# Wider transposes, a u product over two tiles and bias rows on ScalarE, in a retention and gated-MLP kernel bound by TensorE

## The chip, the cores and the metric

The kernel runs on one core of a Trainium2 chip. The metric is the device time of one execution in microseconds (us); lower is better. The kernel before takes 233.5 to 236 us, depending on which chip and in which set of runs. A time below is the median of the runs of its set, slow ones (over 1.5% above the fastest of the same kernel) included. Most sets also ran the kernel before on the same chip in turn with the new one, and only such ratios, of the means of fast runs alone, are compared across sets.

Engines are named as the profile does: PE is TensorE doing matmuls, PEld is TensorE loading weights, DVE is VectorE, ACT is ScalarE, POOL is GpSimd, SP is SyncE, which starts the loads and stores (SPq in the page's list of DMA issues).

## The reference

Eight sequences of 576 positions and eight heads of width 64 go through causal retention (scores weighted by a power of a decay per head, no softmax). The result, 512 wide, goes through a gated MLP whose gate mixes along the sequence.

```python
def _attn_ref(q, k, v):                       # (8, 8, 576, 64) each
    scores = scale * np.matmul(q, k.transpose(0, 1, 3, 2))
    Dmat = np.where(rel >= 0, gamma[:, None, None] ** rel[None, :, :], 0.0)
    return np.matmul(scores * Dmat[None], v)

def _moe_ref(x, w_in, g_ln, w_sg, b_sg, w_out):   # x: (8, 576, 512)
    h = gelu_tanh(x @ w_in)                   # d_ff 1024
    u, v = h[..., :512], h[..., 512:]
    v_n = layernorm(v) * g_ln
    v_s = np.einsum('ts,bsd->btd', w_sg, v_n) + b_sg[None, :, None]
    return x + (u * v_s) @ w_out
```

(Shortened: the decay, the gelu and the layer norm are written by name.)

## The kernel before

The work is cut into blocks of 256 positions (two tiles of 128) and single blocks, five to a pair of sequences. Per block: load q, k, v; multiply q and v by decay factors (GpSimd); transpose q and k on PE; scores, masks, state and output of the retention; then the MLP's hv (the v half), hu (the u half), wp (the product along the sequence) and op (the output). Names in the profile are these tile names; pp is the PSUM tile of transposes, scores and retention output.

A job is one such piece on one engine. A list of job numbers, found beforehand by a search against a timing model, gives the order of issue on each engine. The parts that the change touches:

```python
# transposes: one per 64x64 tile; R picks the input half, C the output half
for a in (1, 0):
    for kk in range(KK):
        for s in range(ns):
            o = ((a * KK + kk) * ns + s) * 64
            for r in range(2):
                for c in range(2):
                    R, C = slice(64 * r, 64 * r + 64), slice(64 * c, 64 * c + 64)
                    ins = nc.tensor.transpose(tpf[C, r, o:o + 64], qkb[R, s, a, KK * c + kk, :], ident[R, R])

# u: one job for one tile of 128 positions, 16 matmuls of 128 columns
for c in range(KK):
    for kk in range(KK):
        ins = nc.tensor.matmul(hu[:, c, :], w_in[:, kk, 128 * c:128 * c + 128],
                               xTs[p][:, kk, 128 * m:128 * m + 128], start=(kk == 0), stop=(kk == KK - 1), ...)

# bias rows: six small copies on VectorE
for t in vmid:
    nc.vector.tensor_copy(t[0][NB0:NB0 + 4, :], row4b[:, 0, :F2])
    nc.vector.tensor_copy(t[1][0:4, :], row4b[:, 0, :F2])

# what a job of u waits for: the half of xT that holds its tile
xd = [J["x", b, s]] if ns == 2 else [J["x", b, 0], J["x", b, 1]]
```

Of the kernel before, what the change touches and what calls it, by code (L numbers as in the profile page):

```python
# [18 lines left out]
OVL = {"PE": 0.0, "DVE": 60.0, "ACT": 90.0, "POOL": 50.0, "SP": 0.0}  # L19
SWITCH = {("F", "Q"): 93.0, ("Q", "F"): 125.0}  # L20
# [4 lines left out]
    '1 0 2 80 81 6 82 f9 83 7 84 f4 85 111 112 87 8 88 f3 114 86 113 3 115 9 89 118 283 120 12 116 119 284 285 286 '  # L25
    '117 23 121 90 f6 287 123 122 288 124 289 13 290 f6 304 127 305 125 4 5 306 126 307 f3 291 128 296 292 15 11 10 '
    '16 308 293 14 297 309 129 294 310 298 17 311 312 301 295 24 315 313 136 303 314 320 25 316 299 302 130 321 317 '
    '18 132 19 32 133 318 20 f3 319 134 21 131 135 22 34 322 300 327 325 328 326 105 329 91 330 137 106 93 323 33 92 '
    '331 94 324 109 332 99 138 110 139 35 100 333 103 97 334 104 98 336 26 366 140 335 101 27 367 95 145 337 107 36 '
    '102 368 108 143 37 141 96 369 144 f1 338 147 342 339 38 355 343 344 142 346 146 356 370 347 154 148 345 28 371 '  # L30
    '387 149 372 340 353 373 341 41 374 31 354 29 150 152 30 151 155 379 40 375 350 388 153 380 156 357 39 351 376 '
    '381 389 358 352 157 163 43 390 437 158 391 377 438 44 392 396 384 378 161 397 159 162 165 439 49 385 401 440 160 '
    '386 398 402 52 164 393 399 441 172 394 166 395 42 174 458 442 167 459 348 443 382 444 349 58 400 445 383 170 403 '
    '446 168 171 460 46 360 461 190 404 169 48 363 405 361 447 414 45 364 179 421 415 450 422 362 406 173 451 47 462 '
    '407 452 479 175 480 463 365 416 464 181 176 359 423 465 51 417 466 424 53 412 455 467 410 413 180 468 408 456 '
    '448 411 457 50 409 469 449 453 188 470 474 454 182 57 475 189 520 183 177 521 471 54 431 178 472 473 186 432 481 '
    '522 187 476 482 433 523 418 484 483 199 477 541 184 191 419 185 542 488 420 478 206 56 192 485 489 524 55 486 '
    '195 487 197 525 425 527 196 526 533 426 207 528 427 534 531 198 529 530 428 532 490 535 200 429 591 538 491 201 '
    '193 430 434 194 592 492 540 496 539 493 543 497 435 593 436 204 594 544 205 494 546 217 498 545 208 495 60 555 '
    '499 61 550 59 556 552 551 612 553 202 209 66 613 203 547 210 500 548 64 507 549 511 508 554 62 595 512 501 213 '  # L40
    '557 596 614 214 597 502 615 513 224 602 559 503 65 598 599 603 604 73 215 600 558 509 601 222 536 605 510 606 '
    '568 537 514 569 609 560 515 216 564 611 561 516 223 218 72 565 610 633 211 219 231 562 634 212 63 577 78 575 578 '
    '616 563 67 576 220 617 221 674 619 517 618 79 625 675 518 620 626 232 519 225 621 68 635 676 226 636 677 240 566 '
    '638 70 637 607 622 567 229 608 627 234 233 572 230 642 235 573 630 574 639 643 242 632 579 631 238 227 580 239 '
    '695 640 241 623 581 696 641 570 249 624 71 504 228 69 628 571 74 505 644 582 629 506 645 76 588 583 678 589 584 '
    '236 679 745 590 237 681 251 646 746 663 680 647 690 664 250 682 691 650 683 747 651 697 748 684 243 698 766 244 '
    '265 699 687 767 700 704 688 247 267 705 689 768 245 769 701 248 709 702 692 246 654 710 648 703 694 749 655 693 '
    '649 252 750 253 258 585 260 661 586 652 751 662 587 259 685 75 653 752 77 706 686 787 707 254 256 255 788 658 '
    '257 656 659 753 660 657 770 708 266 754 261 755 771 711 668 772 262 773 671 276 669 713 670 268 712 263 828 269 '
    '756 672 829 673 264 720 757 731 721 714 732 729 715 270 730 830 789 271 831 274 724 777 725 722 778 275 718 723 '  # L50
    '716 719 761 717 758 762 736 759 760 739 737 763 738 733 740 741 764 779 734 774 765 735 780 782 775 742 783 776 '
    '272 781 743 790 849 792 273 665 744 784 850 791 796 666 785 667 832 786 277 833 797 278 793 834 726 835 794 841 '
    '727 795 728 836 842 798 281 837 279 282 844 799 839 280 845 800 840 838 815 801 851 816 843 806 852 807 846 808 '
    '853 810 854 809 858 848 811 847 855 859 860 856 804 857 861 817 805 863 862 818 802 865 864 825 803 867 812 826 '
    '866 827 822 813 872 814 823 874 873 824 878 875 868 879 870 869 819 871 887 820 821 880 888 889 876 881 883 877 '
# [9 lines left out]
class Job:  # L65
    def __init__(self, eng, dur, due, fn, deps=(), new=None, uses=(), mode=None, nbytes=0, run=0, what="", behind=None, since=0.0, lag=0.0):
        self.what, self.behind, self.since, self.lag = what, behind, since, lag
        self.eng, self.dur, self.due, self.fn = eng, dur, due, fn
        self.deps = [d for d in deps if d is not None]
        self.new = [] if new is None else list(new) if isinstance(new, (list, tuple)) else [new]  # L70
        self.mode, self.nbytes, self.run = mode, nbytes, run
        self.start = self.out = None
        for b in uses:
            b.users.append(self)
        for b in self.new:
            b.users.append(self)


class Planner:


    def __init__(self, bufs, free, slack=60.0, penalty=500.0, fill=None, fill_until=0.0):
# [5 lines left out]
        self.mode, self.warm = None, False  # L88

# [5 lines left out]
    def ready(self, j):  # L95
        t = max(self.free[j.eng], j.since)
        if j.behind is not None:
            if j.behind.start is None:
                return None
            t = max(t, j.behind.start + 100.0)  # L100
# [23 lines left out]
    def place(self, j, t):  # L124
# [15 lines left out]
        else:  # L140
            j.out = t + j.dur
            self.free[j.eng] = t + j.dur - OVL[j.eng]
# [69 lines left out]
def kernel(  # L212
# [64 lines left out]
    garg = consts.tile([128, 2, NBK * 2, H], F32, name="garg")  # L277
    gqv = consts.tile([128, 2, NBK * 2, H], F32, name="gqv")
# [16 lines left out]
    for h in range(H):  # L295
        nc.vector.tensor_scalar(garg[:, 0, :, h], srow[:].rearrange("p n s -> p (n s)"), lng[h], lsc,
                                op0=Alu.mult, op1=Alu.add)
    nc.vector.tensor_scalar(garg[:, 1, :, :], garg[:, 0, :, :], -1.0, lsc, op0=Alu.mult, op1=Alu.add)
    nc.scalar.activation(gqv[:].rearrange("p a m h -> p (a m h)"), garg[:].rearrange("p a m h -> p (a m h)"), Act.Exp)
# [9 lines left out]
    def fill(n, cold):  # L309
# [6 lines left out]
        return Job("PE", 216.0 * n + cold, 0.0, f, new=bf, mode="F")  # L316
# [16 lines left out]
    def win_load(half):  # L333
# [15 lines left out]
        for a, eng, dur in ((0, "DVE", 690.0), (1, "ACT", 1060.0)):  # L349
            jw[half, a] = add(eng, dur, 0.0, lambda a=a, eng=eng: g(a, eng), deps=[ld], uses=[bf], what=("winc", half, a))  # L350
# [40 lines left out]
    st = {}  # L391
# [17 lines left out]
    def a_prep(b, t):  # L409
# [3 lines left out]
        src = f_[:, :, :ns * D].rearrange("p h (s d) -> p s h d", s=ns)  # L413
        if t in "qk" and (b, "qkb") not in st:
            st[b, "qkb"] = new("qkb", [128, 2, 2, H, D], BF)
        if t == "k":
            if b == 0:
                nc.scalar.activation(st[b, "qkb"][:, :ns, 1], src, Act.Copy)
            else:
                nc.gpsimd.tensor_copy(st[b, "qkb"][:, :ns, 1], src)  # L420
            return
        if t == "v":
            st[b, "vb"] = new("vb", [128, 2, H, D], BF)
            dst = st[b, "vb"][:, :ns]
        else:
            dst = st[b, "qkb"][:, :ns, 0]
        a = 0 if t == "q" else 1
        eng = nc.vector if b == 0 and t == "q" else nc.gpsimd
        for s in range(ns):
            eng.tensor_tensor(dst[:, s], src[:, s],  # L430
                                    gqv[:, a, 2 * n + s, :].unsqueeze(2).to_broadcast([128, H, D]), op=Alu.mult)
# [25 lines left out]
    def a_T(b):  # L457
# [7 lines left out]
        for a in (1, 0):  # L465
            for kk in range(KK):
                for s in range(ns):
                    o = ((a * KK + kk) * ns + s) * 64
                    for r in range(2):
                        for c in range(2):  # L470
                            R, C = slice(64 * r, 64 * r + 64), slice(64 * c, 64 * c + 64)
                            ins = nc.tensor.transpose(tpf[C, r, o:o + 64], qkb[R, s, a, KK * c + kk, :], ident[R, R])  # L472
                            n += 1
                            if n == 4:
                                mark(ins, ("T", b))
# [49 lines left out]
    def a_Z(b, c, first):  # L525
# [7 lines left out]
        for kk in range(KK):  # L533
            for s in range(ns):
                for hh in range(2):
                    ins = nc.tensor.matmul(z[64 * hh:64 * hh + 64, kk, :], st[b, "qkb"][R, s, 1, KK * hh + kk, :],  # L536
# [96 lines left out]
    def m_stats(i, first, slot):  # L633
        if first:
            cur["mv"] = new("mv", [128, 2, 4], F32)
        mvs[i] = (cur["mv"], slot)
        bst = sb.tile([128, 6], F32, name="bst", tag="bst", bufs=3)
        nc.vector.bn_stats(bst[:], vgs[i][:])  # L638
        nc.vector.bn_aggr(cur["mv"][:, slot, 0:2], bst[:])  # L639
# [21 lines left out]
    def m_U(i):  # L661
        p, m = divmod(i, NT)
        if m == 0:
            uTs[p] = new("uT", [128, KK, NT * 128], BF)
        hu = psD.tile([128, KK, 128], F32, name="hu", tag="d")
        cur["hu", i] = hu
# [338 lines left out]
```

## Time and profile before

| | before |
|---|---|
| time | 234.21 us (3 runs, 232.78 to 237.35) |
| PE busy | 88% of 233.9 us |
| PE instructions in the built program | 8927, of which 2304 are transposes with their loads and 1152 are u with its loads |
| holes on PE that the prediction puts down to instruction fetch | 9.85 us, ten holes |
| first wp product, last end on PE | 44.83 us, 228.76 us |

The prediction below shows the page's totals, the holes and the blocks of 256 instructions. First the page's PE and clock digits in 40 slices of 5.85 us (9 is 90% or more; the clock is the share of full speed that was granted):

```profile
PE   6638988869869998999989979999999999999991
PEclk9997999997999999999999999999999999999999
```

The clock stands at 7 in two slices. The second, from 52 us, is this stretch in the windows view (stretch, length, busy time and count of PE, PEld, DVE, ACT, POOL, then granted clock, DMA share, GB/s):

```profile
52.00:55.40 3.40, 3.18 (x12) 1.51 (x10) 1.52 (x3) 2.59 (x5) 3.10 (x4) 0.50 1.01 247
55.40:58.00 2.60, 2.60 (x45) 1.50 (x45) 2.04 (x2) 1.47 (x3) 0.00 (x0) 1.00 0.31 87
```

For 3.40 us TensorE ran at half speed, and then at full speed again. By my estimate that lost half of the stretch, 1.7 us. PE's timeline (start, length, engine, line, operation, out<-in, rows*columns of the array, sizes, count, and in brackets the idle time before it):

```profile
48.12 0.62 PE L557 MATMUL pp<-ret,vb 64*64 64x128 bf16 x32
48.57 0.59 PE L472 MATMUL pp<-ident,qkb 64*64 64x64 bf16 x49
51.01 0.32 PE L472 MATMUL pp<-ident,qkb 64*64 64x64 bf16 x15 [1.85 <-issue]
```

The first row ends at 48.74 and the second starts at 48.57: they overlap by 0.17 us, so transposes follow the other 64x64 matmuls without a stop. The transposes are then cut after 49 of 64.

### The profile page before, as it was taken

To read this page: it belongs to the slowest core of one execution; us is meant where nothing else is said; L and a number is where in the kernel's file an instruction comes from. 1 tells how busy PE (TensorE), PEld (TensorE's weight loads), DVE (VectorE), ACT (ScalarE), POOL (GpSimd) and SP (SyncE) were. 2 spreads that over 40 slices of the span, in tenths; PEclk is the share of its full clock that TensorE was granted. 3 is DMA by queue.
4 is the path that set the end of the run, shared out by engine and by line. 5 is a ranking of instruction groups with operands and counts; after the bars stand their busy time and mean duration, and the time that the engine had idled before them with its cause. 6 is when DMAs were issued, how large, how long until landed. Compare 5 with 4: busy or idle time off the path is not lost.

```text
span 233.9 us, 9967 instructions
## 1 busy us (share of the span) xinstructions
PE 205.4 (88%) x4428; PEld 145.1 (62%) x4463; DVE 135.7 (58%) x246; ACT 134.6 (58%) x235; POOL 118.1 (51%) x188
## 2 busy tenths in 40 slices
PE   6638988869869998999989979999999999999991
PEld 1326567654647685668657666677768757667660
DVE  6995746855457746567647484368487416654320
ACT  3013996526567665778376537767655378865431
POOL 5480378984644992976088298457447022222000
PEclk9997999997999999999999999999999999999999
DMA  6999999996498996432997896960262032100333
GB/s 166 290 352 244 259 252 278 337 245 158 134 272 210 301 310 182 117 125 94 298 303 161 218 312 193 238 221 3 81 193 95 0 137 92 48 3 0 135 137 137
DMA packets 70062, 42.88 MB, mean 183 GB/s; under 512 B 14138, under 2 KB 63298, under 8 KB 70018
## 3 DMA queue, kind: packets, MB, share of 16 engines
q1 hardware_dynamic: 70000, 42.23, 65.0%
q8 instruction: 35, 0.57, 1.1%
q14 instruction: 9, 0.07, 0.1%
q10 hardware_dynamic: 18, 0.00, 0.0%
HBM read 32.79 MB, written 9.44 MB: 181 GB/s over the span
## 4 chain that ended last, share of the span: by engine, by line
PE 75%; ACT 7%; DVE 7%; issue 7%; POOL 1%; POOLq 0%; ACTq 0%; DVEq 0%
PE wp L687 17%; PE hu L669 12%; PE op L713 12%; PE hv L624 11%; PE pp L557 6%; PE pp L472 5%; PE op L708 4%; PE pp L504 3%; PE zp L536 3%; PE wtp L782 1%; ACT vg L631 1%; ACT xT L613 1%; PE scr L315 1%; DVE bst L638 1%; DVE ret L517 1%
## 5 line engine op out<-in xcount | busy, mean ns | idle before, releaser
L517 DVE TENSOR_TENSOR ret<-pp,msk 128x1024 bf16<-128x1024 f32 x32 | 38.2, 1216 | 22.4 <-PE pp L504 22.4
L430 POOL TENSOR_TENSOR vb<-ld,gqv 128x512 bf16<-128x512 f32 x36 | 37.3, 1053 | 10.5 <-DMA ld<-in_v_dram 6.1
L687 PE MATMUL wp<-wT,vn 128*128 128x288 bf16 x256 | 41.4, 290 | 0.4 <-ACT uT L678 0.4
L430 POOL TENSOR_TENSOR qkb<-ld,gqv 128x512 bf16<-128x512 f32 x34 | 34.8, 1043 | 13.5 <-DMA ld<-in_q_dram 7.6
L697 DVE TENSOR_TENSOR uT<-wp,uT 128x288 bf16<-128x288 f32 x64 | 28.3, 451 | 20.2 <-PE wp L687 19.0
L669 PE MATMUL hu<-xT,w_in 128*128 128x128 bf16 x576 | 37.5, 219 | 2.8 <-issue 2.8
L669 PEld LDWEIGHTS <-w_in 128*128 128x128 bf16 x576 | 33.9, 98 | 6.5 <-issue 3.6
L613 ACT ACTIVATE xT<-pp 128x512 bf16<-128x512 f32 (+1 forms) x40 | 24.9, 673 | 20.3 <-PE pp L557 20.3
L638 DVE BATCH_NORM_STATS2 bst<-vg 128x6 f32<-128x512 f32 x36 | 24.7, 686 | 20.4 <-ACT vg L631 20.3
L624 PE MATMUL hv<-w_in,xT 128*128 128x512 bf16 x126 | 34.6, 385 | 1.7 <-issue 0.5
L713 PE MATMUL op<-w_out,uT 128*128 128x512 bf16 x130 | 34.3, 379 | 1.3 <-issue 0.5
L481 DVE COPY qkT<-pp 128x2048 bf16<-128x2048 bf16 (+1 forms) x20 | 22.3, 1113 | 20.5 <-PE pp L472 20.3
L643 POOL TENSOR_SCALAR mv<-mv 128x2 f32<-128x2 f32 (+1 forms) x20 | 4.5, 224 | 58.4 <-DVE mv L639 30.0
L718 ACT ACTIVATE ob<-op 128x512 f32<-128x512 f32 x36 | 21.1, 594 | 19.8 <-PE op L713 19.8
L678 ACT ACTIVATE uT<-hu 128x512 bf16<-128x512 f32 x36 | 21.3, 595 | 17.4 <-PE hu L669 17.3
L687 PEld LDWEIGHTS <-vn 128*128 128x128 bf16 x256 | 24.6, 99 | 9.0 <-issue 0.6
L631 ACT ACTIVATE vg<-hv 128x512 f32<-128x512 f32 x36 | 21.3, 595 | 11.5 <-PE hv L624 7.4
L658 ACT ACTIVATE vn<-vg,mv 128x512 bf16<-128x512 f32 x32 | 24.9, 809 | 3.5 <-POOL mv L646 3.4
L420 POOL CAST qkb<-ld 128x1024 bf16<-128x1024 f32 (+1 forms) x19 | 17.9, 949 | 8.8 <-DMA ld<-in_k_dram 4.7
L624 PEld LDWEIGHTS <-xT 128*128 128x128 bf16 x144 | 13.2, 99 | 13.3 <-ACT xT L613 1.0
L545 ACT ACTIVATE zb<-zp 128x256 bf16<-128x256 f32 x32 | 12.2, 381 | 15.8 <-PE zp L536 13.0
L687 PE MATMUL wp<-wT,vmid 128*128 128x288 bf16 x64 | 18.7, 292 | 0.0
(78 smaller groups left out, 253.6 us busy)
## 6 DMA issues: line engine op xcount, KB each, us to landing
out_dram<-ob SPq DMA_DIRECT2D x36, 256.0 KB, 2.2
ld<-in_k_dram SPq DMA_DIRECT2D x16, 512.0 KB, 7.3
ld<-in_q_dram SPq DMA_DIRECT2D x16, 512.0 KB, 7.9
ld<-in_v_dram SPq DMA_DIRECT2D x16, 512.0 KB, 7.2
wst<-in_moe_w_in_dram SPq DMA_DIRECT2D x2, 1024.0 KB
wst<-in_moe_w_sg_dram SPq DMA_DIRECT2D x2, 576.0 KB, 4.0
ld<-in_q_dram SPq DMA_DIRECT2D x8, 128.0 KB, 4.6
ld<-in_k_dram SPq DMA_DIRECT2D x8, 128.0 KB, 4.6
```

Of the source, the lines that this page charges most:

```text
L430: eng.tensor_tensor(dst[:, s], src[:, s], gqv[:, a, 2 * n + s, :].unsqueeze(2).to_broadcast([128, H, D]), op=Alu.mult)
L481: ins = nc.vector.tensor_copy(st[b, "qkT"][:].rearrange("p c a k t -> p c (a k t)")[:, :, :w], st.pop((b, "tp"))[:].rearrange("p c a k s t ...
L517: ins = nc.vector.tensor_tensor(ret[:].rearrange("p r (k t) -> p (r k) t", k=2), sc[:].rearrange("p r (k t) -> p (r k) t", k=2), msk2[:].r ...
L613: nc.scalar.activation(dst, src, Act.Copy)
L624: ins = nc.tensor.matmul(hv[:], xTs[p][:, kk, 128 * m:128 * m + 128], w_in[:, kk, F2:], start=(kk == 0), stop=(kk == KK - 1))
L631: unfence(nc.scalar.activation(vgs[i][:], cur.pop(("hv", i))[:], Act.Gelu_apprx_tanh), ("V", i))
L638: nc.vector.bn_stats(bst[:], vgs[i][:])
L658: nc.scalar.activation(vn[:], vg[:], Act.Identity, scale=mv[:, s, 2:3], bias=mv[:, s, 3:4])
L669: ins = nc.tensor.matmul(hu[:, c, :], w_in[:, kk, 128 * c:128 * c + 128], xTs[p][:, kk, 128 * m:128 * m + 128], start=(kk == 0), stop=(kk ...
L687: ins = nc.tensor.matmul(ps[:], vns[t0 + j][e][:, 128 * c:128 * c + 128], wT[e][j][:, half * HS:(half + 1) * HS], start=(j == 0), stop=(j ...
L697: ins = nc.vector.tensor_tensor(uTs[p][:, c, col:col + HS], cur.pop(("wp", b, c, half))[:], uTs[p][:, c, col:col + HS], op=Alu.mult)
L713: ins = nc.tensor.matmul(op[:], uTs[p][:, c, r], w_out[:, c, :], start=False, stop=(c == KK - 1), skip_group_check=True)
```

## The change

Four things are meant to make PE's program shorter and its start earlier.

- A transpose takes 64 rows and 128 columns of weights (two heads) at a time: half as many. q and k are laid out for that when they are prepared.
- u is computed for both tiles of a block in one matmul of 256 columns. One job makes half of the channels for two tiles.
- The bias rows are placed by ScalarE.
- The order is searched again, with a model that counts PE's instructions and charges 4.8 us for each block of 256.

```diff
+FETCH = 4800.0
+            if j.eng == "PE":
+                while self.count + j.ins > 256 * self.block:
+                    at = t + j.dur * (256 * self.block - self.count) / j.ins + late
+                    late += max(0.0, self.landed - at)
+                    self.landed = max(self.landed, at) + FETCH
...
                     for r in range(2):
-                        for c in range(2):
-                            R, C = slice(64 * r, 64 * r + 64), slice(64 * c, 64 * c + 64)
-                            ins = nc.tensor.transpose(tpf[C, r, o:o + 64], qkb[R, s, a, KK * c + kk, :], ident[R, R])
+                        R = slice(64 * r, 64 * r + 64)
+                        ins = nc.tensor.transpose(tpf[:, r, o:o + 64], qkb[R, a, kk, s].rearrange("p c d -> p (c d)"), ident[R, R])
...
-    def m_U(i):
+    def m_U(i, w, half):
+        cs = range(KK) if w == 1 else range(2 * half, 2 * half + 2)
+        for n, c in enumerate(cs):
             for kk in range(KK):
-                ins = nc.tensor.matmul(hu[:, c, :], w_in[:, kk, 128 * c:128 * c + 128],
-                                       xTs[p][:, kk, 128 * m:128 * m + 128],
+                ins = nc.tensor.matmul(hu[:, n, :], w_in[:, kk, 128 * c:128 * c + 128],
+                                       xTs[p][:, kk, 128 * m:128 * m + 128 * w],
...
+        xd = [J["x", b, 0], J["x", b, 1]]
...
         for t in vmid:
-            nc.vector.tensor_copy(t[0][NB0:NB0 + 4, :], row4b[:, 0, :F2])
-            nc.vector.tensor_copy(t[1][0:4, :], row4b[:, 0, :F2])
+            nc.scalar.activation(t[0][NB0:NB0 + 4, :], row4b[:, 0, :F2], Act.Copy)
+            nc.scalar.activation(t[1][0:4, :], row4b[:, 0, :F2], Act.Copy)
```

(Left out are the order list, the new layout of the decay factors and of q and k, the other row copies, and bookkeeping of the u jobs.)

## The prediction

The sum: -0.7 (u) - 7 (fetch) + 4 (modes) - 2 (bias rows) - 1.5 (order) = -7.2, so 234.2 became 227.0 us. In rival (1) "near 232" stands without support, and of rival (4), slower writes of GpSimd, nothing in the trace spoke; the 0.04 for "slower" rested on it alone. A mode is the shape of the array that the timeline prints for a matmul (128*128, 64*128 or 64*64). A drain is the overlap that is missing where the mode changes: 0.08 us at the change quoted, for 0.16 to 0.20 between neighbours of one mode. What PE does there no trace shows. The 56 ns of a 128-column step is the usual one; the shortest in the trace is 55.

> **What bounds the kernel now.** I read the page first, then the groups by shape, the chain in order of time, and the windows and timeline around its waits.
>
> ```profile
> PE 205.4 (88%) x4428; PEld 145.1 (62%) x4463; DVE 135.7 (58%) x246; ACT 134.6 (58%) x235; POOL 118.1 (51%) x188
> DMA  6999999996498996432997896960262032100333
> q8 instruction: 35, 0.57, 1.1%
> PE 75%; ACT 7%; DVE 7%; issue 7%; POOL 1%; POOLq 0%; ACTq 0%; DVEq 0%
> ```
>
> The first line is each engine's busy time and instruction count, the second the DMA share in 40 slices of 5.85 us, the third one row of the DMA queues, the last the chain that ended last. TensorE is the bound: 75% of the chain (some 175 us) is matmuls, no other engine is over 58% busy, and after about 55 us the timeline shows PE almost without a hole. Before that the DMA digits stand at 9, PE runs fill matmuls, and the start is set by loads and by VectorE. "Issue", 7% or some 16 us, is time in which PE waited for no semaphore. The long pieces of it (start us, us, what):
>
> ```profile
> 43.15 1.11 issue
> 49.16 1.85 issue
> 62.31 0.94 issue
> 68.24 1.75 issue
> 117.55 1.04 issue
> 136.12 1.16 issue
> ```
>
> With 0.74 at 91.74, 0.32 at 95.89, 0.55 at 142.67 and 0.39 at 158.80 they sum to 9.85 us. What they are, the windows from the end of one such hole to the start of the next show (columns: stretch, length, PE and PEld busy with counts, then DVE, ACT, POOL, clock, DMA share, GB/s):
>
> ```profile
> 44.20:49.15 4.95, 4.89 (x128) 3.77 (x128) 3.64 (x7) 0.72 (x1) 4.75 (x5) 1.00 1.05 295
> 63.20:68.20 5.00, 4.90 (x127) 3.61 (x128) 2.37 (x3) 3.88 (x7) 3.61 (x4) 1.00 1.02 278
> 92.45:95.60 3.15, 3.07 (x125) 2.38 (x127) 1.24 (x2) 2.73 (x7) 2.98 (x6) 1.00 0.25 91
> ```
>
> Each stretch holds 128 + 128 = 256 instructions, a few records missing. PE stops after 256 instructions, in the middle of a job: the hole at 49.16 cuts the 64 transposes of one block into 49 and 15. And the instruction queue moved 35 packets in 0.57 MB, 16.4 KB or 256 x 64 bytes each, for 4428 + 4463 = 8891 PE instructions, which are 35 blocks. So these 9.85 us are **instruction fetch**. A block plus its hole took 4.95 + 1.85 = 6.8 us with the DMA full, but 3.15 + 0.32 = 3.5 us with it a quarter busy.
>
> [...] neighbours of one mode overlap by 0.16 to 0.20 us, the full-array matmul ending at 48.06 and the 64x64 one starting at 47.98 by 0.08 us, so a switch costs about 0.1 us. [...] the trace has 98 ns for a 128x128 load against 109 ns for a 64x64 one[...]. [...]
>
> ```profile
> 11.32 1.04 DVE L770 COPY vmid<-row4b 4x512 bf16<-4x512 bf16 x1
> 12.37 1.03 DVE L771 COPY vmid<-row4b 4x512 bf16<-4x512 bf16 x1
> 13.42 1.03 DVE L770 COPY vmid<-row4b 4x512 bf16<-4x512 bf16 x1
> 14.46 1.03 DVE L771 COPY vmid<-row4b 4x512 bf16<-4x512 bf16 x1
> 17.79 0.30 DVE L774 COPY wT<-row4b 4x576 bf16<-4x576 bf16 x1
> ```
>
> The four placed while GpSimd multiplies (8.9 to 16.4 us) take 1.03 us, a wider one after it 0.30 us.
>
> **The change part by part.**
>
> Transposes. Two 64x64 ones become one 64x128 one: 1152 matmuls become 576, with their loads 1152 instructions fewer. The stream need not shrink: 64 of them span 0.71 us in the timeline with a latency of 0.197 us for the last, so 0.51 us, or 33 ns per four tiles that run together. Now two run together, each again streaming 64 columns of the identity. 16 pairs at 33 ns are the same 0.53 us. I take 0.
>
> u product. 576 matmuls of 128 columns become 320: 256 of 256 columns for the 16 blocks of two tiles, and 64 of 128 for the single tiles. That is 512 instructions fewer. A step is 56 ns at 128 columns and 122.5 ns at 288 (0.61 us for 5), so by the line through both 109 ns at 256. Eight at 109 are 0.87 us against 16 at 56, 0.90 us: 32 halves x 0.02 = **-0.7 us**.
>
> Fetch. In the built programs PE goes from 8927 rows to 7275 (1664 less, 12 more for fills): 28.4 blocks for 34.9, 19% fewer, and most of what goes stood in the densest bursts, 128 instructions in 0.53 us. The order was also searched with 4.8 us per block in its model, so it should spread the rest. That constant lies between the 3.5 and 6.8 us above, so it is too kind while the DMA is full, where 5.65 of the 9.85 us were lost (the four holes up to 70 us). I leave 3 us: **-7 us**.
>
> Tiling modes. The 64x128 mode is a third one. Going through the PE order and counting neighbours, before has 84 changes between full array and the rest, and transposes beside other small matmuls cost nothing. After has 94 such changes and 31 between transposes and 64x64 matmuls. 41 x 0.1 us = **+4 us**, all on PE's path. The planner's own model still gives the transpose the old mode, so its search did not avoid these.
>
> Bias rows. The four copies held VectorE from 11.32 to 15.49 us, on the chain, ahead of the first mask multiply (15.42). ScalarE was idle from 6.2 to 12.0 and 13.4 to 20.0 us; four at the 0.59 us that it takes for 512 elements hide there. The first mask multiply can come 3.5 us earlier. The first half of w_in is also queued ahead of the second block's v. But until about 54 us GpSimd waits for loads whose rate the full DMA sets, so I count about half: **-2 us**.
>
> Q/k/v preparation. One GpSimd instruction for two of 1.05 us over half the elements saves little, and GpSimd is off the chain after the start: 0. New order otherwise, fewer short waits: **-1.5 us**, a guess.
>
> Sum: -0.7 - 7 + 4 - 2 - 1.5 = -7.2. 234.2 - 7.2 = **227.0 us**.
>
> **The rivals.** (1) *Drains eat the gain.* If each transpose job also pays more for its weights, [...] the total stays near 232. For it: a 128-column step never goes below 56 ns in this trace, so nothing shows the load to be faster. Against: the 98 against 109 ns. (2) *The DMA becomes the bound of the first 80 us.* Its share there is 0.84 to 1.05, and PE made faster would then wait for q, k, v instead of for instructions. For it: GpSimd's waits for loads until 54 us. Against: over the span the queue is 65% busy and drops after 80 us, so PE catches up later with work it has in store. It would leave only the fetch holes after 80 us (4.2 us) and give about 231. (3) *All goes well:* 64x64 to 64x128 is no drain, fetch vanishes and the early 3.5 us carry to the end: -10 - 4 - 1 - 1 gives 218. [...]
>
> **Range and chances.** The two big terms oppose each other and each is uncertain by 3 to 4 us, the early one by 2, so about 5 us in all: 221 to 232.5 us for 8 in 10. Faster by over 2% means under 229.5, which 227 passes by half a standard deviation and a bit: 0.71. Within 2%: 0.25, mostly by rivals 1 and 2. Slower: 0.04, rival 4.
>
> **What would show each step right or wrong.** Fetch: 28 or 29 packets in the instruction queue, and issue pieces over 0.3 us on the chain that sum to about 3 us; over 6 would refute it. Transposes: 32 in about 0.7 us in the timeline[...]. Modes: a matmul beside a transpose of the other shape overlapping its neighbour by under 0.1 us; 0.17 or more means no drain. u: eight matmuls in 0.87 us plus latency. Bias rows: the vmid copies on ScalarE near 0.6 us and the first mask multiply near 12 us; the first big product wp several us before 44.8 us shows the early gain carried, at 43 or later that the loads ate it. If PE shows waits for loads or for qkb after 55 us, rivals 2 or 4 hold. The prediction is wrong if TensorE isn't the bound, or if the time falls outside the range by a term not listed here.

## The result, and the profile after

The changed kernel took **223.98 us** (median of 4 runs, 222.67 to 224.68) against 233.53 for the kernel before in the same set. The ratio is 0.9595, with a 95% interval of 0.954 to 0.965: faster, and inside the predicted range.

The page after: totals, PE, clock and DMA digits, the instruction queue, and the chain that ended last.

```profile
PE 206.7 (93%) x3599; PEld 140.9 (63%) x3637; DVE 129.7 (58%) x239; ACT 138.7 (62%) x241; POOL 113.3 (51%) x157
...
PE   7689699899999999999999999998999999999992
...
PEclk9999999999999999999999999999999999999999
DMA  6999799999999999999898021599010111211333
...
q8 instruction: 28, 0.46, 0.9%
...
PE 76%; SPq 8%; DMA 5%; issue 3%; DVE 2%; ACT 2%; POOL 1%; ACTq 0%
```

PE has 19% fewer instructions and is still busy for the same time, 206.7 us for 205.4, but now that is 93% of a shorter span. Seven instruction packets are gone. The clock has no digit below 9. The DMA stands at 9 for longer: its main queue moves the same 42.23 MB in a shorter span. "Issue" is 3% of the chain; before it was 7%. Its pieces over 0.3 us in the chain in order of time (start, us):

```profile
31.23 0.54 issue
...
36.79 0.49 issue
...
134.43 0.46 issue
...
153.78 0.83 issue
...
191.91 0.46 issue
```

Only the one at 153.78 is a hole on PE at a block boundary; in the others the chain is on another engine. PE's own idle times show one more fetch hole, 0.29 us at 98.47. So 1.1 us of fetch holes are left, where before lost 9.85.

The transposes beside retention matmuls, in PE's timeline:

```profile
45.11 0.62 PE L575 MATMUL pp<-ret,vb 64*64 64x128 bf16 x32
45.66 0.64 PE L490 MATMUL pp<-ident,qkb 64*128 64x64 bf16 x32
46.23 0.31 PE L575 MATMUL pp<-qkT,zb 64*64 64x128 bf16 x8
```

Thirty-two take 0.64 us; before, 64 took 0.71. The overlap with the neighbours is 45.73 - 45.66 = 0.07 us and 46.30 - 46.23 = 0.07 us, where before had 0.17. So by these ends a change costs about 0.1 us at each side. It is no single case: in the complete trace of the same kernel (x9 below) all 31 such neighbours overlap by 0.067 to 0.071 us, and in x6, the same order with narrow transposes, all 91 by 0.165 or more. (The ends of matmuls are modelled by the profiler.)

One half of the u product of a block, and what follows it:

```profile
60.88 1.04 PE L689 MATMUL hu<-xT,w_in 128*128 128x256 bf16 x8
61.75 0.39 PE L729 MATMUL op<-ident,xT 128*128 128x128 bf16 x4
```

The next work starts 0.87 us after it. And the bias rows, in the timelines of ACT and then of DVE:

```profile
11.32 0.63 ACT L791 ACTIVATE vmid<-row4b 4x512 bf16<-4x512 bf16 x1
...
13.24 0.63 ACT L792 ACTIVATE vmid<-row4b 4x512 bf16<-4x512 bf16 x1
```

```profile
10.25 1.22 DVE L499 COPY qkT<-pp 128x2048 bf16<-128x2048 bf16 x1
12.08 2.35 DVE L535 TENSOR_TENSOR ret<-pp,msk 128x1024 bf16<-128x1024 f32 x2 [0.60 <-PE pp L522]
```

The first mask multiply moved from 15.42 to 12.08 us. The first wp moved from 44.83 to 42.15.

**Where the time went.** From first wp to the last end on PE took 183.93 us before and 176.23 after, 7.70 less. Adding up what the traces show for that stretch: fetch holes 8.74 to 1.12 (-7.6), the half-speed window (-1.7), 0.004 us for each of some 290 transpose steps (-1.1 at most), u (-0.6), and 29 more changes of tiling mode (+2.9, at the 0.1 us above): -8.1, 0.4 us more than was measured. (Of the 41 more changes that the prediction counted, 29 between transposes and 64x64 matmuls lie in this stretch; the ten more between full array and the rest all lie before it.) The other 2.68 us came before first wp.

**One trace is one draw.** The half-speed time differs from execution to execution. The timed runs of before beside x1 to x12, 25 in all, have mean granted clocks from 0.953 to 0.984; those of the changed kernel have 0.997 to 1.0. A straight line through the 25 gives 1.3 us for each hundredth of the clock (correlation 0.75). With mean clocks of 0.974 and 0.999 this makes some 3 us of the gain go with the clock. It is an estimate from an association, and larger than the 1.7 us of the profiled run.

### The profile page after: what moved, and what is told of

The parts are those of the page before. It is cut to its first block, busy times and chain, and to the rows that moved or that the text cites. A ratio compares the mean times of both kernels' runs of the same rounds, so it can differ in the third digit from the quotient of the medians.

```text
span 222.3 us, 8281 instructions
## 1 busy us (share of the span) xinstructions
PE 206.7 (93%) x3599; PEld 140.9 (63%) x3637; DVE 129.7 (58%) x239; ACT 138.7 (62%) x241; POOL 113.3 (51%) x157
## 3 DMA queue, kind: packets, MB, share of 16 engines
q1 hardware_dynamic: 70000, 42.23, 68.8%
## 4 chain that ended last, share of the span: by engine, by line
PE 76%; SPq 8%; DMA 5%; issue 3%; DVE 2%; ACT 2%; POOL 1%; ACTq 0%
PE wp L708 17%; PE op L734 13%; PE hu L689 13%; PE hv L642 12%; PE pp L575 6%; SPq L425 5%; PE op L729 4%; PE pp L522 4%; PE pp L490 4%; DMA wst<-in_moe_w_sg_dram 3%; PE zp L554 3%; DMA ld<-in_q_dram 2%; SPq L355 2%; SPq L422 2%; DVE ret L535 1%
## 5 line engine op out<-in xcount | busy, mean ns | idle before, releaser
L450 POOL TENSOR_TENSOR vb<-ld,gqv 128x1024 bf16<-128x1024 f32 (+1 forms) x20 | 34.5, 1730 | 18.0 <-DMA ld<-in_v_dram 11.3
L708 PE MATMUL wp<-wT,vn 128*128 128x288 bf16 x256 | 40.9, 286 | 0.1
L450 POOL TENSOR_TENSOR qkb<-ld,gqv 128x1024 bf16<-128x1024 f32 (+1 forms) x19 | 32.7, 1721 | 12.5 <-PE wtp L803 4.9
L689 PE MATMUL hu<-xT,w_in 128*128 128x256 bf16 (+1 forms) x320 | 36.8, 262 | 2.1 <-ACT xT L631 1.3
L642 PE MATMUL hv<-w_in,xT 128*128 128x512 bf16 x128 | 35.2, 380 | 1.0 <-issue 0.2
L734 PE MATMUL op<-w_out,uT 128*128 128x512 bf16 x128 | 33.8, 379 | 0.8
L689 PEld LDWEIGHTS <-w_in 128*128 128x128 bf16 x320 | 28.2, 98 | 9.8 <-issue 2.6
L734 PEld LDWEIGHTS <-uT 128*128 128x128 bf16 x144 | 12.6, 98 | 8.5 <-DVE uT L718 0.2
```

Of the source, the lines that this page charges most:

```text
L450: eng.tensor_tensor(dst, src, g.unsqueeze(3).to_broadcast(list(src.shape)), op=Alu.mult)
L642: ins = nc.tensor.matmul(hv[:], xTs[p][:, kk, 128 * m:128 * m + 128], w_in[:, kk, F2:], start=(kk == 0), stop=(kk == KK - 1))
L689: ins = nc.tensor.matmul(hu[:, n, :], w_in[:, kk, 128 * c:128 * c + 128], xTs[p][:, kk, 128 * m:128 * m + 128 * w], start=(kk == 0), stop= ...
L708: ins = nc.tensor.matmul(ps[:], vns[t0 + j][e][:, 128 * c:128 * c + 128], wT[e][j][:, half * HS:(half + 1) * HS], start=(j == 0), stop=(j ...
L734: ins = nc.tensor.matmul(op[:], uTs[p][:, c, r], w_out[:, c, :], start=False, stop=(c == KK - 1), skip_group_check=True)
```

## The experiments

All kernels below gave correct results. "Rows" is the number of instructions in PE's built program. A fetch hole is counted only where PE stops at its instruction 193 + 256 k, the place of the block boundaries in all these traces, and only after the first wp. PE's weight loads, matmuls and sequencer instructions are counted for this. In the twelve traces without missing records every wait of PE put down to "issue" lies within one instruction of such a place. The last column but one is time at half clock between first wp and the last end on PE. The wait for xT counts the waits of u for it over the whole run.

| run | what it is | us, median | ratio to before | rows | fetch holes, us | half clock, us | u waits for xT, us |
|---|---|---|---|---|---|---|---|
| before | | 233.5 to 236 | 1 | 8927 | 8.7 | 3.4 | - |
| after | the change | 223.98 | 0.9595 | 7275 | 1.1 | 0 | 1.3 |
| x1_old_order | the change, order of before | 226.92 | 0.9677 | 7263 | 0 | 0 | 3.9 |
| x2_new_order | after, with the transposes, u columns and rows of before | 240.3 | 1.0225 | 8939 | (slow) | (slow) | - |
| x3_t_only | before + wide transposes | 227.32 | 0.9663 | 7775 | 2.1 | 0 | - |
| x6_64_transposes | after - wide transposes | 233.33 | 0.9928 | 8427 | 7.9 | 3.4 | 1.6 |
| x4_u_only | before + wide u | 234.33 | 1.0003 | 8415 | 5.3 | 3.4 | 3.2 |
| x5_rows_only | before + rows on ScalarE | 232.59 | 0.9915 | 8927 | 8.9 | 0 | - |
| x7_128_u | after, u in 128 columns | 222.52 | 0.9496 | 7787 | 0 | 0 | - |
| x8_rows_dve | after, rows on VectorE | 226.92 | 0.9661 | 7275 | 1.5 | 0 | 1.3 |
| x9_after_again | after, once more | 222.68 | 0.9483 | 7275 | 1.1 | 0 | 1.3 |
| x10_128_u_again | x7 once more | 222.46 | 0.9484 | 7787 | 0 | 0 | - |
| x11_after_shift | x9, 84 more instructions at 6 us | 222.39 | 0.9476 | 7359 | 0.2 | 0 | 1.3 |
| x12_128_u_shift | x10, 84 more instructions at 6 us | 227.51 | 0.9670 | 7871 | 3.7 | 3.4 | - |

One run of x3, of x8 and of x12 and two of x2 were slow. Before the first wp, and from the first record of the clock on (4.2 us in before, 6.1 in after), before spent 3.4 us at half clock in its trace, x1 and x5 6.8 us, x3, x4 and x8 10.2 us, and the other fast traces none. It bears on what can be read from the start (see x5 and x8).

Read down by rows, the holes fall from 7.9 to 8.9 us at 8427 to 8927 rows (5.3 at 8415) to 0 to 3.7 at 7775 to 7871 and 0 to 1.5 at 7263 to 7359. So the trend does not rest on one place of the block boundaries. Whether the count matters, or how densely the instructions are packed, no run separates.

The theory: fewer PE instructions mean fewer and shorter fetch holes, and this is nearly all of the gain; it comes from the transposes, in spite of the drains. The rivals: the new order does it; the u product or the early start does it; the drains eat the transposes' part.

### The transposes: x3 and x6

```diff
 before
-    two 64x64 transposes for each half and head pair
+    one 64x128 transpose, with the layout of q and k that it needs
```

> Kernel before with the 64x128 transposes alone (1152 PE instructions fewer, 30 to 31 blocks, 27 mode changes that were none before). Theory A: holes fall by about 6 us, drains cost 2.7, the stream is 1.1 shorter: about 229 us. Rival, drains eat the gain: 232 us or more.

```diff
 after
-    tpf[:, r, o:o + 64], qkb[R, a, kk, s] (both heads)
+    for c in range(2): tpf[C, r, o:o + 64], qkb[R, a, kk, s, c, :]
```

> Changed kernel with its transposes 64x64 again, same layout and order (8428 PE rows, 31 mode changes gone). Theory A: about 5 us of fetch holes come back, drains of 3.1 go, the stream is 1.1 longer: about 227 us. Rival, drains weigh as much as fetch: 224 us or less.

Alone, in the old order, the wide transposes bring 0.9663 (0.956 to 0.976): 227.32 us. Taken out of the changed kernel they leave 0.9928 (0.985 to 1.001), 233.33 us, which is as good as nothing. The chains in order of time tell why; first x3, then x6, pieces of "issue" from 40 us on that are over 0.6 us:

```profile
50.46 0.74 issue
...
67.41 0.69 issue
...
149.54 0.70 issue
```

```profile
44.18 0.75 issue
...
48.52 2.61 issue
...
97.23 2.40 issue
...
156.16 0.88 issue
...
161.19 1.23 issue
```

With the wide transposes three short holes remain, and with the narrow ones in the new order five come, two of them longer than any of before. All eight lie at block boundaries. x6 also has a half-speed window again, 3.4 us at 0.50 from 50.8 us, just after its hole at 48.52. From first wp to the last end on PE, x6 took 183.04 us and the changed kernel 176.23, 6.8 less: holes -6.7, half clock -1.7, transpose steps -1.1, 29 drains +2.9 make -6.6. For x3 against before, -7.4 measured: holes -6.6, half clock -1.7, transpose steps -0.9, 24 drains +2.4 make -6.8. In both the sum fits within 0.6 us. Without the drains it would miss by 1.8 to 2.7 us. So the drains are paid and the transposes win all the same; the rival of the eaten gain falls. Theory A had the sign in both, but for x6 it foresaw 227 us: 6.7 us of holes came, not 5, and the half-speed window with them.

### The order alone, and the change in the old order: x1 and x2

```diff
 after: ORDER
-    the new list
+    before's list (with the u jobs of a block in place of those of its tiles)
```

> All four parts of the change, in the order of the kernel before (7264 PE rows for 8927, 27 changes between the 64x128 and the 64x64 mode). Theory A, fewer instructions remove the fetch holes: holes fall from 9.9 to about 3 us, drains add 2.7, transposes and u give 1.8, the start 2: about 225.5 us, 28 instruction blocks. Theory B, it is the newly searched order that pays: over 230 us, close to before.

```diff
 after: three of the four parts taken out
-    transposes 64x128; u in 256 columns; rows on ScalarE
+    transposes 64x64; u in 128 columns; rows on VectorE
```

> The new order with the old instruction counts: transposes 64x64, u in steps of 128 columns, bias rows on VectorE (8940 PE rows, 35 blocks, no drain between transposes and the other small matmuls). Theory A: fetch holes stay at 7 us or more, about 230 us. Theory B: the search with fetch in its model spreads the instructions, holes under 3 us, about 226 us.

All parts in the old order give 226.92 us, 0.9677 (0.962 to 0.974). The new list with the old instruction counts gives 240.3 us (239.7 for the three fast runs alone), 1.0225 (1.013 to 1.032): above before in every fast run, though unclear by the rule of 2%. Both theories, 230 and 226 us, missed. (It keeps the new layout of q, k and v and the u jobs for two tiles, so it is not the old kernel with a new list alone.) Its profiled run was slow, so its holes are not compared here, only the timed fast runs, and why it is so slow stays open. So the order is no gain by itself: it goes with the program it was searched for. What it adds to the change is some 2 to 4 us: x1 has a ratio of 0.9677, the changed kernel had 0.9595 and 0.9483 in its two sets.

What x1 loses is not fetch: it has no fetch hole after the first wp. In its view of waits (engine and tile, what it waited for: us in total, times, longest) the first row is

```profile
PE hu L690 <- ACT xT L632: 3.9, 5, 1.9
```

u of a block now needs both halves of xT. The old order was made for a u that needs one half, and PE stands at u five times. In the new order it does so once, for 1.3 us.

### The u product: x4, x7, and again x9 to x12

```diff
 before
-    16 matmuls of 128 columns for each tile
+    8 of 256 columns for both tiles of a block, twice
```

> Kernel before with the u product over both tiles alone (512 PE instructions fewer, no new tiling mode, 33 blocks). Theory A, with what the transposes alone gave for 1152 instructions: about half of the holes' gain for half the instructions, 3 us, and 0.7 us of stream: about 231 us. Rival, u gives its stream alone and holes only move: 233 to 234 us.

```diff
 after: m_U
-    hu[:, n, :] over 128 * w columns
+    for t in range(w): hu[:, n, 128 * t:128 * t + 128] over 128 columns of tile m + t
```

> Changed kernel with u in steps of 128 columns again (same jobs and order, 512 PE instructions more, 7788 rows). Theory A: 2 to 3 us of fetch holes come back and 0.7 us of stream: about 227 us. Rival: only the stream, 224.7 us.

u alone brings nothing: 1.0003 (0.995 to 1.006), as its rival said. Its fetch holes fell from 8.7 to 5.3 us, by what 512 fewer rows might save, but the view of waits has a new row:

```profile
PE hu L672 <- ACT xT L614: 3.2, 4, 1.5
```

3.2 us of new waits against 3.4 us of holes: the same dependency as in x1. The prediction had not seen it.

Taking u's part out of the changed kernel (x7, 512 rows more) did not cost the microseconds that I had expected; 222.52 us was even less than the 223.98 of the changed kernel, though in another set on another chip. x7 had no fetch hole after first wp and no wait of u for xT. Was that better code, or luck in where the block boundaries fell? Four runs on one chip, five rounds each, were to tell: both kernels again, and both with 84 extra instructions in a fill at 6 us, where PE waits anyway, so that every boundary falls 84 instructions earlier in the work.

> The changed kernel again, word for word, on the chip and beside the runs of x10, so that the two can be compared. The wider u product helps or is neutral: 223 to 225 us, within 0.3% of x10 or below it. The u product hurts: 224, about 1% above x10. Also tells how far a kernel moves between chips: 223.98 before.

> The changed kernel with u in steps of 128 columns again, as in x7, which took 222.52 us. If x7 was luck of one chip: 224 or more, no better than x9. If steps of 128 are really as good or better in this order: 222 to 223, ratio to x9 0.990 to 0.996, and again no instruction hole on PE after 45 us.

```diff
 after, and x10: the second fill, at 6 us
-    6 matmuls of 512 columns
+    48 matmuls of 64 columns
```

> The changed kernel with 48 matmuls of 64 columns in place of 6 of 512 in one fill at 6 us, where PE waits anyway: 84 more instructions, so every 256-instruction boundary falls 84 instructions earlier in the work; the work after 9 us is the same. Theory A, x7's lead over the changed kernel is where the boundaries fall: the three holes of about 1.5 us and the hu wait of 1.30 us move or go, and the time changes by 1 us or more either way (222 to 222.8 if they go, 225 to 227 if longer ones come), at another place than 98, 153 and 192 us. Theory B, the 256-column u costs by itself (the wait at 25 us, longer blocks of one kind of work): 224 as in x9, within 0.7 us, with the hu wait still 1.3 us.

> x10 with the same shift of 84 instructions. Theory A, where the boundaries fall: x10 had no hole after 45 us by luck, so the shift can only cost: 223.5 to 227, with holes of 0.3 to 2.5 us on PE at block boundaries. Theory B, 128-column steps are better by themselves: 222 to 223 as x10, about 1% under x11.

On one chip the two are equal: 222.68 and 222.46 us, 0.9483 and 0.9484. x7's lead was the set, not the kernel. The shift does nothing to the changed kernel (222.39 us) and costs the one with narrow u 4.4 us by the means of fast runs (227.51, 0.9670). Its chain in order of time, "issue" from 40 us on:

```profile
49.20 1.61 issue
...
126.11 0.35 issue
...
137.42 0.46 issue
...
153.03 0.68 issue
...
158.05 1.03 issue
```

All but the one at 137.42 are PE holes at block boundaries, 3.7 us together; x10 has none there. After the first of them the windows view shows:

```profile
51.30:54.70 3.40, 3.40 (x22) 2.31 (x20) 1.47 (x2) 0.60 (x1) 1.80 (x1) 0.50 1.13 280
```

3.40 us at half clock cost another 1.7, by the same estimate. Together 5.4 us; from first wp to the last end on PE x12 took 6.2 us more than x10 (its first wp came 1.2 us earlier), so 0.8 us is not accounted for. The work after 9 us is the same in both. So the narrow u was as good only where its boundaries fell well. Neither of the two theories written down was right alone. Theory A (boundaries decide) holds for the narrow u, where the shift costs 4 to 5 us. For the wide u the holes moved (1.15 us at 22.75 came, those at 53 and 98 us went) but the time did not. The wait of 1.3 us for xT stayed in x9 and x11, as Theory B had it, yet costs nothing in total: first wp comes at 41.6 us with it and at 42.1 in x10 without it. What u's part brings is 0 at one place of the boundaries and 2% at another. Two places are too few to give a mean.

### The bias rows: x5 and x8

```diff
 before: place_vmid, place_wT
-    nc.vector.tensor_copy(...)
+    nc.scalar.activation(..., Act.Copy)
```

> Kernel before with the bias rows placed by ScalarE alone. The first mask multiply moves from 15.4 to about 12 us. Theory A: the gain is partly eaten by the loads, the fetch holes stay, 1 to 2 us faster than before. Rival, loads set the start in any case: no difference, within 0.5 us.

> Changed kernel with the bias rows on VectorE again, in its order. Theory A: [...] the first big product starts 1 to 3 us later and the end about 2 us later: 226 us. Rival, loads set the start: within 0.5 us of the changed kernel.

(x8 is the same edit of the changed kernel, backwards. Measured is that in before the four vmid copies took 1.03 to 1.04 us each while GpSimd was multiplying and the wider wT copies 0.30 after it. In x8 the vmid copies stood later, from 14.96 us on, and took 0.28 to 0.29 us.) Alone the rows bring 0.9915 (0.986 to 0.997), about 2 us, and all of before's holes stay, 8.9 us. But the trace of x5 does not show these 2 us as an earlier start. Its first mask multiply begins at 11.88 us, 3.5 us sooner, and at 31 us the lead is 3.6 us. Then it is lost. GpSimd waits for a load of v, and PE for GpSimd (GpSimd of before, then GpSimd and PE of x5):

```profile
33.09 1.04 POOL L430 TENSOR_TENSOR vb<-ld,gqv 128x512 bf16<-128x512 f32 x1 [0.49 <-DMA ld<-in_v_dram]
...
32.26 1.04 POOL L430 TENSOR_TENSOR vb<-ld,gqv 128x512 bf16<-128x512 f32 x1 [3.29 <-DMA ld<-in_v_dram]
...
33.35 0.26 PE L557 MATMUL pp<-ret,vb 64*64 64x64 bf16 x2 [2.71 <-POOL vb L430]
```

Before has this product at 35.78, so 2.4 us of the lead are left. But x5 is at half clock from 32.36 to 39.18 us, and the next u product starts at 40.07 against 40.13. First wp comes at 44.32, 0.5 us sooner, because the fetch hole before it is 0.4 us shorter. So at the start the load took 1.2 us of the lead and the half clock 2.4. Another 1.1 us lie after first wp, where before has its half-speed window and x5 has none. How much of the rows' lead was left thus went with the clock in these two traces.

In the changed kernel putting the rows back on VectorE gives 226.92 us, 0.9661 (0.957 to 0.975); x7, on the same chip and as fast as the changed kernel where both ran, had 222.52, so they are worth some 4 us there by the means of fast runs. In VectorE's timeline of x8 the two wT copies take 1.61 and 1.91 us from 10.27 us on, while GpSimd multiplies, and the copy of qkT starts after them, at 13.72 instead of 10.25. PE waits 3.36 us for it, and first wp comes at 46.70 instead of 42.15: 4.55 us, of which all is left at the end (last end on PE 222.89 against 218.38). But this execution, at 228.54 us and a clock of 0.976, is the longest of x8's fast runs, with 10.2 us at half clock from 14.5 us on. The two others took 225.2 and 225.3 us at 0.992, so without that stretch the rows may be worth nearer to 3 us.

### What beats what

No variant beats the changed kernel. The two that came nearest and ran beside it on the same chip, x10 and x11, lie within 0.2% of it, which is no difference at the spread of these runs (221.4 to 224.3 us).

## Why the prediction was right, step by step

The time was right, 223.98 us for 227.0 with a range of 221 to 232.5, and the chance of "faster" stood at 0.71. The mechanism was the one named. The 3 us of difference are terms that were mis-sized (fetch, modes, order), one that was left out (the clock) and one wait not foreseen.

- **Fetch, -7.** 28 packets, as foreseen. The holes fell by 8.7 us over the run (9.85 to 1.1), because 1.1 us stayed and not 3. That is the mechanism, confirmed by x3 (2.1 us left) and x6 (7.9 us back). The sign that the prediction gave for it, pieces of issue on the chain of about 3 us in sum, came out at 2.8, but by luck: four of the five pieces are no holes of PE. The time that a block takes went with the DMA here too. Where two holes follow each other by one block (x5, x6, x11, x12), from the end of one to the end of the next it is 5.4 to 7.7 us at a DMA share of 0.95 to 1.10, 4.6 at 0.85 and 3.7 at 0.29. But part of the size is luck: 84 instructions at 6 us moved 3.7 us of holes into the narrow-u kernel, so this term is known to a few us at best for any one program.
- **The clock, not listed.** Before's 3.4 us at half speed from 52 us cost 1.7 us, and after has none. In before, x4, x6 and x12 a hole near 49 us (1.85, 3.34, 2.61 and 1.61 us) is followed by such a window; x3 and the changed kernel have no such hole there and no window. A hole of 1.85 us at 48.65 in x5, one of 1.75 at 68.24 in before and one of 2.40 at 97.23 in x6 have no window after them. In before the recorded clock changes at 17.83, 21.24, 51.96, 55.38 and 232.87 us, steps of 1, 9, 1 and 52 times 3.413 us, so on one grid. The half-speed stretches of the other traces that are named here have the length of one to three such steps (3.4 us in x4, x6 and x12, 6.8 in x5, 10.2 in x8), at another place in each execution. The windows view, laid on that grid, for before, x12, x8 and the two stretches that share x5's hole (length, then PE's busy time):

```profile
48.55:51.96 3.41, 1.56 (x107) 1.36 (x96) 0.97 (x3) 0.48 (x1) 2.38 (x3) 1.00 0.94 238
...
47.87:51.28 3.41, 1.80 (x64) 1.47 (x62) 2.17 (x4) 2.24 (x5) 2.62 (x3) 1.00 1.20 218
...
96.42:99.83 3.41, 1.87 (x53) 1.24 (x53) 2.71 (x4) 2.50 (x5) 2.90 (x4) 1.00 1.22 242
...
46.01:49.42 3.41, 2.64 (x102) 2.04 (x100) 2.42 (x5) 0.00 (x0) 3.41 (x4) 1.00 1.16 291
49.42:52.83 3.41, 2.33 (x52) 1.81 (x53) 1.88 (x3) 1.85 (x4) 2.24 (x3) 1.00 1.00 176
```

  Counted between the first wp and the last end on PE of all the fast traces, the four stretches in which PE was busy for 1.80 us or less (before, x4, x6, x12) were followed by half clock, and no stretch with 1.87 or more was. The three holes without a window are each cut in two by a line of the grid (x5's into 0.77 and 1.08 us). So in these traces the 1.7 us went with where a hole fell on the grid. This is an association, since no run moved the grid, and no limit can be read from so few stretches; and before the first wp, where PE works in short pieces, it is not so clean (x7 has 1.62 us busy and stays at full clock, x1 has 2.10 and falls).
- **Tiling modes, +4.** The missing overlap is there: it fell from 0.17 to 0.07 us beside a transpose, so a change costs 0.1 us, and the sums for x3 and x6 close only with them. The size is nearer to +3: of the 41 changes, "all on PE's path", 12 come before the first wp, where PE waits for other things. No run measured the drains by themselves; the neighbours in x9 and x6 are the closest to it.
- **Transposes, 0.** Thirty-two start to start take 0.45 us (0.64 less the latency of the last, 0.19), 29 ns for a pair (31 steps), where four 64x64 ones took 33. About -1.1 us in all. The dearer weights of rival 1 are not there: a load for 64x128 took 95 ns, one for 64x64 109.
- **u, -0.7.** The stream is right (0.87 us for eight). As a part of the total it is wrong in kind: the step assumed that only the stream and the instruction count change. But one matmul now reads both tiles, which needs both halves of xT. x4 and x1 show 3.2 and 3.9 us of waits for that in the old order; in the new order 1.3 us are left, at a place where it costs nothing.
- **Bias rows, -2.** First wp came 2.7 us earlier in the changed kernel. In the new order the rows are worth some 3 to 4 us (x8). In the old order (x5) more than the half that the prediction took off was given back: a load of v took 1.2 us of the lead, as it foresaw, and a half-speed stretch, which it did not list, 2.4. So the hit of 2 us in x5's time is in part luck: 1.1 us of it lie after first wp, where the half-speed window is missing.
- **Q/k/v preparation, 0.** One GpSimd multiply of 1024 elements now takes 1.90 us where two of 1.05 us stood. Rival 4 did not come.
- **Order, -1.5, a guess.** x1 says 2 to 4 us. In the two traces it pays by spreading the u jobs' waits, not by the fetch: x1 has no fetch holes after first wp. With x2 it is no term that can be added to any program.

Of the rivals, (2) "the DMA becomes the bound" can be seen in the digits, where the DMA stands at 9 for longer, but PE had other work and did not wait for loads after 55 us. (3) had its parts half: fetch all but vanished and the changed kernel's earlier start carried to the end, but the drains came.

## What to carry to other kernels

In these traces PE's fetch holes lay where its program crossed blocks of 256 instructions (9.85 us in before, 1.1 in after), so count the instructions of the busiest engine, find those places and read the "issue" holes there. Where dense bursts of small matmuls (128 instructions in 0.53 us) met a full DMA queue (a share of 1.0), half as many transposes paid more than their stream (x3: 0.9663, of which the stream is 0.9 us by the sum above) and paid for 24 extra changes of mode at 0.1 us. A merged matmul waits for the later of its inputs (3.2 us of new waits in x4, 3.9 in x1), so ask for each merge what it now waits for. Look at the clock after a hole as well: after four holes of 1.61 to 3.34 us here it stood at 0.50 for 3.4 us, and after three others of 1.75 to 2.40 us it did not fall. And do not judge a part of a few us from one program (84 instructions in an idle place moved the narrow-u kernel by 4.4 us, x12 against x10, and the changed kernel by none, x11 against x9): shift the instruction stream by some dozens in such a place and time it again, on the same chip.
